# Attention units of one segment, two chunks at a time: a planned order laid out anew

## The chip, the cores and the metric

The kernel runs on one core of a Trainium2 chip. The metric is the device time of one execution in microseconds; several runs of a kernel are given by their median. A profile is taken of one further execution. The engines are named as in the profile: PE is the matrix engine, with its weight loads shown apart as PEld; DVE, ACT and POOL are the vector, scalar and general engines; SP issues nearly all DMAs.

## The reference

A sequence of 2048 rows of 512 goes through attention with a compressive memory and then through a gated feed-forward block, each behind a layer norm without weights and each with a residual:

```python
h  = x + attention(layernorm(x))          # wq, wk, wv, wo: 512 x 512, 32 heads of 16
h2 = h + ffn(layernorm(h))                # 512 -> 1376 -> 512, gelu(gate) * up
```

Attention works in four segments of 512 rows. Within a segment it is causal softmax attention. Each head also reads a memory of the earlier segments and then adds its own segment to it:

```python
a_dot = softmax(q k^T / 4 + causal mask) v
a_mem = (phi(q) M) / (phi(q) z + 1e-6)    # phi(t) = t + 1 for t > 0, else exp(t)
o = g * a_mem + (1 - g) * a_dot           # g = sigmoid(beta), one per head
M, z = M + phi(k)^T v, z + sum(phi(k))    # after each of the segments
```

So segment s of a head needs the memory that segment s-1 of the same head left. All is in float32.

## The kernel before

**Precision.** A large product is made of three: each operand is split into a rounded high part and a low part, and high-high, high-low and low-high are summed (`SPLIT`). Weights are split on ACT (high part) and on POOL or DVE (low part) by `split_weight` and `split_wv`.

**Units.** Eight heads form a chunk `c` (0 to 3). The 16 units of attention are the pairs (chunk, segment), and `UNITS` lists them in the order in which they are worked. Before, the first half takes chunk 0 with segments 0 and 1, chunk 1 with segments 0 and 1, and so on; the second half does the same with segments 2 and 3. For each unit `qkv(U)` projects q and k (24 matmuls, L653; for unit 0 both together at L665), splits them on ACT (L735) and DVE (L739), and moves the parts by DMA into the layouts that the score products want: three DMAs of q (L750) and six of k (L756) per half unit, issued by SP. `vproj` (L694) makes v for two chunks at a time, in the units whose chunk is even. If a later segment wants the memory, `qkv` also makes phi(k) (L673 to L677), transposes it (L773), multiplies it with v (L781) and adds it up (L788 to L796). `mem(U)` reads the memory for segments above 0: the denominator (L811), its inverse on DVE (L817 to L819), the product (L827) and the multiplication (L829).

**Passes.** A unit has two halves of four heads, numbered Q = 2U and 2U + 1. `pass_a(Q)` computes scores with queries on the rows (L855) for their maxima alone, which DVE takes out of the banks (L863); the maxima are transposed (L886), copied (L889) and written by a small DMA into the q operand (L891). `pass_b(Q)` computes the scores again with keys on the rows and the maxima subtracted by the product itself (L920, L928), ACT takes the exponential (L936), POOL cuts the triangle (L939), and PE multiplies with v in four column strips (L960). The result is copied (L981), goes through HBM, is divided and joined with the memory's part (L984 to L1006), and goes to `o_dram`.

**What sets the order.** The whole program is written out by a list planner, `Sched.run`, as the kernel is built. Each step is an operation with an engine, a duration, a priority, and the values that it reads and writes; buffers and banks come from pools. The planner takes the step that can begin first and, among those that can begin within 0.059 us of it, the one of the lowest priority. The priorities come from the unit's number plus a due time of each step out of the table `DUE` ("q", "k", "d", "v", "m" per unit; "a", "b", "p", "o" per half; "w" for the output projection and "l" for the first layer norm per segment). The real engines then run their instructions in that order and wait where data is late.

**Written over the plan by hand.** In some places the code issues an instruction at another place than the planner put it. `AHEAD` names five halves whose maxima DMA is marked `urgent`: it is issued ahead of the next DMA of SP once it is possible. `BEHIND` places the first squares of a later layer norm on ACT behind the high part of the first k. The steps of the first layer norm are fused so that the root on ACT and the final normalisation stand where they were wanted. `again` puts up to six matmuls of 512 columns, whose result isn't used, into pass B of the last half (L1116).

**The start.** The rows of segment 0 are loaded and normalised, while 17 transposes whose result isn't used run on PE (L533). The rows are transposed (L602), unit 0's q and k are projected, then v. In the order before, unit 1 is chunk 0 of segment 1, so segment 1's layer norm and its transposes (L613) come right behind. The layer norms of segments 2 and 3 are laid out with units 4 and 5 (`LN1_AT`).

**The end.** `wo_seg` projects a segment's output once all four chunks of it are done (L1033). The second layer norm and the feed-forward products (L1220, L1285) follow; they take over the banks and buffers of attention as these come free.

The weights of the next chunk are split once a unit of an odd segment has been laid out:

```python
        if s % 2 and U < 15:
            h, cn = divmod(U // 2 + 1, NCH)
            for i in range(2):
                W[h, cn, i] = split_weight(2 * (U + 1) + (-3.175), (wq, wk)[i][cn], PW)
            if c % 2:
                split_wv(h, cn // 2, 2 * (U + 1) - 2.4, 3.0)
```

Of the kernel before, what the change touches and what calls it, by code (L numbers as in the profile page):

```python
# [15 lines left out]
P = 128  # L16
D = 512
# [11 lines left out]
UNITS = [(c, s) for h in range(2) for c in range(NCH) for s in (2 * h, 2 * h + 1)]  # L29
# [107 lines left out]
class Sched:  # L137
# [4 lines left out]
    def __init__(self):  # L142
        self.ops, self.urgent = [], set()
# [28 lines left out]
    def run(self, window=0.059, stay=0.1):  # L172
# [5 lines left out]
        while cand:  # L178
# [72 lines left out]
def infini_geglu(ctx: ExitStack, tc: tile.TileContext, x, wq, wk, wv, wo, beta,  # L251
# [29 lines left out]
    def dma(prio, fn, ins, outs, kb=256, dur=None, **k):  # L281
        return S.op("SP", dur or (0.4 if kb == 256 else 0.64), prio, fn, ins, outs, lat=kb / 290, **k)
# [79 lines left out]

    vh = Val(PE_)
# [3 lines left out]
    def c_iota():  # L367

        nc.gpsimd.memset(ones[:, 0:1], 1.0)
        nc.scalar.activation(ones[:, 1:2], ones[:, 0:1], AF.Sqrt)  # L370
# [18 lines left out]
    dve(1000, -9.5, c_mmask, [vh, vj], [vmmask, vh, vj])  # L389
# [7 lines left out]
    pool(0.5, -9, c_ident, [], [vident])  # L397
# [7 lines left out]
    vone, vq0, vk0, vv0 = Val(), [Val() for _ in stq_t], [Val() for _ in stk_t], [Val() for _ in va_t]  # L405

    pool(0.7, -8.5, lambda: None, [vident], [vone])
# [20 lines left out]
    def c_stk(i, after):  # L428
        t = stk_t[i]
        for a in range(2):  # L430
            own, other = slice(64 * a, 64 * a + 64), slice(64 - 64 * a, 128 - 64 * a)
            def fill(a=a):

                if i == 1:
                    if a:
                        nc.scalar.activation(ones[:, 1:2], ones[:, 0:1], AF.Exp)
                    return
                for s, b in [(i, a)] + ([(1, 0), (1, 1)] if i == 0 and a else []):
                    rows = slice(64 * b, 64 * b + 64)
                    nc.scalar.activation(stk_t[s][rows, :, b], one[rows, :, None].to_broadcast([64, 2, D]), AF.Copy)  # L440
            act(2 * D, -4.2 + i, fill, [vone] + after, [vk0[i]], src=0.1, chain=True)
# [32 lines left out]

    BEHIND = None


    def layer_norm(prio, rows, dst, off=False, keep=None, acq=None, done=(), behind=(), scratch=None):
        bn, mv = Val(PBN), Val(PMV)
        y, z = Val(PLN), Val(PLN)  # L480
# [15 lines left out]
        for t in range(4):  # L496
            if off:
# [10 lines left out]
                def squares(t=t, junk=junk):  # L508
                    nc.scalar.activation(junk.t, rows[t].t, AF.Square, bias=bn.t[:, t, 1:2],
                                         accum_out=mv.t[:, t, 1:2])  # L510

                def place(f=squares, late=t == 0 and BEHIND is None):

                    nonlocal BEHIND
                    if late and BEHIND is None:
                        BEHIND = f
                    else:
                        f()
                act(D, prio, place, [rows[t], bn], [junk, mv], src=0.4, chain=True)
            else:  # L520
                def f(t=t):
                    nc.vector.bn_stats(bn.t[:, t], rows[t].t)
                    nc.vector.bn_aggr(mv.t[:, t], bn.t[:, t])
                    if t == 3 and scratch and not behind:

                        nc.vector.tensor_scalar(v_(), mv.t[:, :, 1], 1e-5, None, op0=OP.add)
                        nc.scalar.activation(z.t, v_(), AF.Sqrt)
                dve(840, prio, f, [rows[t], *behind], [bn, mv], chain=True,
                    acq=[v, z] if t == 3 and scratch and not behind else [])
        if done and not behind:  # L530

            wm = Val(PB)
            pe(12 * 0.21, prio, lambda: [nc.tensor.transpose(  # L533
                wm.t[0:6, 0:P], ident[:, 0:6] if n else bn.t[:, 1], ident) for n in range(17)],
                [bn, vident], [wm])
# [17 lines left out]
        def y_():  # L553
            return y.t
        def z_():
# [8 lines left out]
        if done:  # L564
# [4 lines left out]
            n = 4 if behind else 3  # L569
            b = None if behind else Val(PLN)  # L570

            def root():
                nc.vector.reciprocal(y.t, z.t)
                nc.vector.scalar_tensor_tensor(b.t, mv.t[:, :, 0], -1.0, y.t, op0=OP.mult, op1=OP.mult)
                nc.scalar.activation(rows[3].t, rows[3].t, AF.Identity, scale=y.t[:, 3:4], bias=b.t[:, 3:4])
            dve(3500 if behind else 3250, prio, lambda: [
                *[f() for f in ([g, *[f for f, _, _ in steps]] if behind else [root])],
                *[norm(t) for t in range(n)]],
                [mv, *rows, *(HL0 if behind else [])], [v, u, y, z, *([b] if b else []), *rows[:n], *done])
            if b:  # L580
                act(4, prio, lambda: None, [b, y], [rows[3]])
# [17 lines left out]
        if done and not behind:  # L599
# [5 lines left out]
            for dc in range(ND):  # L605
                split_psum(prio, pts[dc], dst[dc])
            return
# [103 lines left out]
    def qkv(U):  # L711
# [11 lines left out]
        for i in range(2):  # L723
# [10 lines left out]
            def high(pm=pm, hl=hl, sc=sc, last=U == 0 and i == 1):  # L734
                nc.scalar.activation(hl.t[:, 0], pm.t, AF.Copy, scale=sc)  # L735
                if last:
                    BEHIND()
            act(D, first, high, [pm], [hl])
# [5 lines left out]
            for h, Q in enumerate(half):  # L744
                dst = (STQ, STK)[i][Q]
                zeros = (vq0, vk0)[i][Q:Q + 1]
                for r, part in enumerate(((0, 1, 0), (0, 0, 1))[i]):
# [6 lines left out]
                    for a in range(2):  # L754
                        dma(moved + 0.2 + h, lambda dst=dst, r=r, part=part, h=h, hl=hl, a=a:
                            nc.sync.dma_start(  # L756
                                dst.t[64 * a + r:64 * a + 64:4, :, a].bitcast(F32),
                                hl.t[64 * h + 32 * a:64 * h + 32 * a + 32, part].bitcast(F32)),
                            [hl] + zeros, [dst], kb=64, chain=True)
# [40 lines left out]
    def mem(U):  # L800
# [23 lines left out]
        spread(prio, r, U, 1, vr)  # L824
        pm = Val(PD)
        om = OM[U] = Val(POM)
# [4 lines left out]
    def spread(prio, r, U, i, vr):  # L831
# [3 lines left out]
            tensor=src.tensor, offset=src.offset, ap=[[0, 16], [D, 8], [1, D]])), [vr], [r], kb=430, dur=0.67)  # L835


    AHEAD = (12, 14, 18, 25, 29)


    def pass_a(Q):
# [51 lines left out]
        if Q in AHEAD:  # L893
            S.urgent.add(S.ops[-1].fn)

    def pass_b(Q):
# [14 lines left out]

        def bank(parts):
# [4 lines left out]
            def f():  # L917
                if kb == 3:
# [4 lines left out]
                    again(Q, kb)  # L923
# [6 lines left out]
                again(Q, kb)  # L930
# [174 lines left out]

    turns = []

    def again(Q, kb):
        if Q < 31 or kb == 0 or len(turns) == 6:
            return  # L1110
        turns.append(kb)
        f = forder[0]
        w, (v, c0) = FW[f], FWS[0, f]["a11"]
        assert banks_of[0, forder[1]][0].t is None
        dst = next(t for t in banks[3:5] if t is not banks_of[0, f][0].t)
        nc.tensor.matmul(dst[:w], v.t[:, 0, c0:c0 + w], B[0]["11"][0].t[:, 0, :], start=True, stop=True,  # L1116
# [271 lines left out]
```

## Time and profile before

| | us |
|---|---|
| median of 3 runs | 828.82 (828.08 to 829.05) |
| the profiled execution | 828.38 |
| its span in the profile | 826.7 |
| PE busy | 808.3 (98%) |
| DVE busy | 611.8 (74%) |
| ACT busy | 564.4 (68%) |
| POOL busy | 484.8 (59%) |

The span runs from the first to the last instruction on the engines; the profiled execution's own time is 1.7 us longer. Busy times of different engines overlap. A group of the profile gives the line, the engine, the operation, what is written and read, the shape and the count; behind the first bar the busy time and the mean length of one instruction in ns; behind the second the idle time of the engine just before them, and what ended it. Matmuls overlap one another, so the mean length of one is more than the distance between two. A line number can be that of a helper which several steps share.

### The profile page before, as it was taken

The numbers are of one execution on the slowest core, as the hardware profiler recorded it, in microseconds if no ns is written. First come the engines' busy times: TensorE is split into PE (matmuls) and PEld (weight loads), VectorE is DVE, ScalarE is ACT, GpSimd is POOL, SyncE is SP. The second block draws the span as 40 slices with busy tenths as digits, with TensorE's granted clock in tenths as the row PEclk, the third lists the DMA queues.
The fourth block names the chain that finished last, engine by engine and source line by source line (L and its number), as shares of the span: only waits on it lengthen the run. The fifth ranks groups of instructions, "written<-read, shape, count | busy, mean of one in ns | idle before, by whom it ended". The sixth has DMA issues, their size and how long they took to land.

```text
span 826.7 us, 15337 instructions
## 1 busy us (share of the span) xinstructions
PE 808.3 (98%) x4721; PEld 626.6 (76%) x4721; DVE 611.8 (74%) x1823; ACT 564.4 (68%) x1131; POOL 484.8 (59%) x720
## 2 busy tenths in 40 slices
PE   7999999999999999999999999999999999999998
PEld 6788777777867767867756587888888787888886
DVE  7889776888878878699985964666568865665665
ACT  8778788889787777876776753787467454546541
POOL 8433443443264454545736885888698676869750
PEclk9999999999999999999999999999999999999999
DMA  7543545655446655564654665431111341211202
GB/s 257 135 129 97 147 125 133 165 145 156 123 128 184 168 146 153 148 163 128 181 182 135 205 192 179 152 116 52 52 52 52 107 151 39 78 39 51 64 1 102
DMA packets 71893, 103.51 MB, mean 125 GB/s; under 512 B 14340, under 2 KB 25156, under 8 KB 71812
## 3 DMA queue, kind: packets, MB, share of 16 engines
q1 hardware_dynamic: 71668, 102.41, 42.4%
q8 instruction: 37, 0.61, 0.3%
q14 instruction: 44, 0.36, 0.1%
q10 hardware_dynamic: 144, 0.13, 0.0%
HBM read 54.92 MB, written 21.43 MB: 92 GB/s over the span
## 4 chain that ended last, share of the span: by engine, by line
PE 51%; DVE 3%; DMA 1%; ACT 1%; issue 0%; SPq 0%; POOL 0%; ACTq 0%; DVEq 0%
PE bank L1220 24%; PE bank L1285 14%; PE bank L1033 5%; PE bank L960 2%; PE bank L855 2%; PE bank L928 2%; PE bank L653 1%; DVE row L596 1%; PE bank L613 1%; DMA row<-o_dram 1%; DMA cd<-pv_dram 0%; DVE bank L1062 0%; PE bank L827 0%; DVE ln L551 0%; DVE aside L863 0%; ACT stk L1068 0%
## 5 line engine op out<-in xcount | busy, mean ns | idle before, releaser
L939 POOL TENSOR_SCALAR_AFFINE_SELECT pt<-pt 128x128 f32<-128x128 f32 (+2 forms) x352 | 119.9, 349 | 173.7 <-ACT pt L936 168.8
L936 ACT ACTIVATE pt<-bank 128x512 f32<-128x512 f32 (+1 forms) x352 | 182.5, 558 | 40.5 <-PE bank L928 28.1
L863 DVE CUSTOM_DVE_ANT_0 bank<-bank,amask 128x512 f32<-128x512 f32 (+1 forms) x256 | 156.7, 637 | 32.2 <-PE bank L855 30.7
L855 PE MATMUL bank<-stk,stq 128*128 128x512 f32 (+2 forms) x384 | 131.1, 383 | 3.4 <-DVE nm L863 2.1
L928 PE MATMUL bank<-stq,stk 128*128 128x384 f32 (+2 forms) x384 | 114.5, 354 | 2.2 <-ACT pt L936 2.1
L653 PE MATMUL bank<-xt,w 128*128 128x512 f32 x360 | 102.9, 395 | 0.0
L855 PEld LDWEIGHTS bank<-stk,stq 128*128 128x128 f32 x384 | 69.2, 188 | 26.6 <-DVE nm L863 10.0
L1293 DVE TENSOR_TENSOR pt<-pt,bank 128x512 f32<-128x512 f32 x95 | 64.1, 686 | 33.0 <-PE bank L1285 33.0
L863 DVE CUSTOM_DVE_ANT_0 aside<-bank,amask 128x256 f32<-128x256 f32 (+1 forms) x256 | 76.7, 353 | 14.8 <-PE bank L855 13.6
L928 PEld LDWEIGHTS bank<-stq,stk 128*128 128x128 f32 x384 | 68.0, 188 | 22.8 <-ACT pt L936 9.0
L960 PE MATMUL bank<-pt,vaug 128*32 128x512 f32 (+3 forms) x1024 | 76.7, 436 | 0.0
L653 PEld LDWEIGHTS bank<-xt,w 128*128 128x128 f32 x360 | 65.2, 188 | 10.1 <-DVE xt L623 0.2
L960 PEld LDWEIGHTS bank<-pt,vaug 128*32 128x32 f32 x1024 | 28.7, 109 | 40.9 <-issue 33.8
L863 DVE DVE_READ_ACCUMULATOR2_ANT nm<- 128x1 f32 x512 | 57.0, 111 | 0.0
L694 PE MATMUL bank<-wv,xt 128*128 128x256 f32 x384 | 55.0, 282 | 0.0
L694 PEld LDWEIGHTS bank<-wv,xt 128*128 128x128 f32 x384 | 51.9, 189 | 1.6 <-DVE mb L790 0.2
L455 POOL TENSOR_TENSOR w<-raw,w 128x512 fp32r<-128x512 f32 x25 | 32.3, 1293 | 29.6 <-ACT w L450 21.5
L1220 PE MATMUL bank<-xt,w 128*128 128x512 f32 (+1 forms) x168 | 46.5, 394 | 0.0
L1190 POOL TENSOR_TENSOR stk<-raw,stk 128x512 fp32r<-128x512 f32 (+3 forms) x28 | 31.1, 1111 | 22.8 <-PE bank L1220 14.5
L1190 POOL TENSOR_TENSOR w<-raw,w 128x512 fp32r<-128x512 f32 (+3 forms) x34 | 38.7, 1142 | 4.3 <-ACT w L1188 3.5
L1220 PE MATMUL bank<-xt,stk 128*128 128x512 f32 (+1 forms) x138 | 38.1, 391 | 0.3 <-ACT pq L1227 0.3
L1220 PE MATMUL bank<-stk,w 128*128 128x512 f32 (+1 forms) x135 | 38.0, 391 | 0.0
(310 smaller groups left out, 1847.7 us busy)
## 6 DMA issues: line engine op xcount, KB each, us to landing
stq<-hl SPq DMA_DIRECT2D x96, 128.0 KB
stk<-hl SPq DMA_DIRECT2D x192, 64.0 KB
pv_dram<-pvs SPq DMA_DIRECT2D x32, 256.0 KB
r<-r_dram SPq DMA_DIRECT2D x28, 256.0 KB
row<-x SPq DMA_DIRECT2D x24, 256.0 KB
raw<-wg SPq DMA_DIRECT2D x20, 256.0 KB
raw<-wu SPq DMA_DIRECT2D x20, 256.0 KB
raw<-wd SPq DMA_DIRECT2D x20, 256.0 KB
```

Of the source, the lines that this page charges most:

```text
L653: nc.tensor.matmul(pm.t, w.t[:, wi, dc * P:(dc + 1) * P], XT[s][dc].t[:, xi, :], start=dc == 0 and n == 0, stop=dc == ND - 1 and n == 2)
L694: nc.tensor.matmul(pm.t[:, 256 * t:256 * t + 256], XT[s][dc].t[:, xi, t0:t0 + P], whl[wi].t[:, h, 256 * (dc % 2):256 * (dc % 2) + 256], st ...
L855: nc.tensor.matmul(sa.t[:, k * w:(k + n) * w].rearrange("x (n w) -> x n w", n=n), sq.t[:, p, i * P:(i + 1) * P], sk.t[:, p, a:a + n, 0:w], ...
L863: nc.vector.tensor_tensor_reduce(out=(sa.t if i > 1 else aside)[:, k * w:(k + 1) * w], in0=sa.t[:, k * w:(k + 1) * w], in1=amask[:, D - w: ...
L928: nc.tensor.matmul(sc.t[:, lo:lo + D - q0], sk.t[:, p, a, q0:q0 + P], sq.t[:, p, q0:D], start=True, stop=True)
L936: act(w, prio, lambda: nc.scalar.activation(e.t[:, :w], sc.t[:, :w], AF.Exp), [sc], [e])
L939: nc.gpsimd.affine_select(v, v, pattern=pat + [[1, P]], compare_op=OP.is_ge, fill=0.0, base=0, channel_multiplier=-1)
L960: nc.tensor.matmul(pv.t[32 * n:32 * n + 32, kb * P:D], va.t[:, 136 * kb + 17 * j:136 * kb + 17 * j + 32], e.t[:, lo:lo + D - kb * P], star ...
L1190: pool(0.14 + 2.13e-3 * (hi - lo), prio, lambda: nc.gpsimd.tensor_tensor(v.t[:, 1, :hi - lo], r.t[:, lo:hi], v.t[:, 0, :hi - lo].bitcast(F ...
L1220: nc.tensor.matmul(dst.t[:w], v.t[:, wi, c0 + j * w:c0 + (j + 1) * w], b[bk][j].t[:, xi, :], start=first and j == 0 and n == 0, stop=j == ...
L1285: nc.tensor.matmul(pm.t[:, cs], HH[p, f, s][hi].t[:w, t * P:(t + 1) * P], v.t[:w, wi, cs], start=f == fl[0] and n == 0, stop=f == fl[-1] a ...
L1293: dve(W_, prio, lambda a=a, pm=pm, cs=cs, to=to: nc.vector.tensor_tensor(to.t[:, cs], a.t[:, cs], pm.t[:, cs], op=OP.add), [pm, a], [to])
```

## The change

`UNITS` takes two chunks of one segment, then the same two chunks of the next segment, then the other two chunks. The table `DUE` is another one throughout. Several durations that the planner reckons with are set to other values: a DMA of less than 256 KB holds SP for 0.68 rather than 0.64, the mask and the identity at the start take longer. What was written over the plan by hand is gone: `urgent`, `AHEAD`, `BEHIND`, and the fused steps of the first layer norm, which are steps of their own now, as are the two loads of ACT's function tables (`vtab`). The fills of the k operands of the first two halves are four ACT steps of one half tile each. For Q = 0, the four DMAs of k's high part (part 0) are issued by ACT, through `by_act`. The dummies at the start are 20 transposes that wait for the second row tile. The fillers in the last pass B are up to ten matmuls of 512 columns, one behind each group of score products once a bank is free. The multiplied memory read's buffer `om` is taken when the denominator is spread, not at the product. Weights are split when the next unit is the first of its chunk in this half.

```diff
-UNITS = [(c, s) for h in range(2) for c in range(NCH) for s in (2 * h, 2 * h + 1)]
+UNITS = [(c, s) for h in range(2) for p in (0, 2) for s in (2 * h, 2 * h + 1) for c in (p, p + 1)]
...
 DUE = {
-    "q": [-4, -4, 1.75, 2.5, 4, -3.75, 2.375, 1.25, 2.25, 4, 1.875, 3.875, 3.5, -3.5, 0.75, 4],
+    "q": [4, 0.25, -0.375, -0.625, 1.875, 2, 0, 2.25, 0.5, 4, 1.375, 4, 1, -2.875, -2.5, 4],
...
-    "l": [0, 0, -1.625, 0.375],
+    "l": [0, 0, 1.75, -0.75],
 }
...
-            if o.eng == "SP":
-
-                for q in cand:
-                    if q.fn in self.urgent:
-                        self.urgent.remove(q.fn)
-                        q.fn()
-                        q.fn = int
-            self.urgent.discard(o.fn)
             o.fn()
...
-        return S.op("SP", dur or (0.4 if kb == 256 else 0.64), prio, fn, ins, outs, lat=kb / 290, **k)
+        return S.op("SP", dur or (0.4 if kb == 256 else 0.68), prio, fn, ins, outs, lat=kb / 290, **k)
+
+    def by_act(prio, fn, ins, outs):
+        S.op("ACT", 0.45, prio, lambda: fn(nc.scalar), ins, outs, lat=2.4, chain=True)
...
-            pe(12 * 0.21, prio, lambda: [nc.tensor.transpose(
-                wm.t[0:6, 0:P], ident[:, 0:6] if n else bn.t[:, 1], ident) for n in range(17)],
-                [bn, vident], [wm])
+            pe(20 * 0.213, prio, lambda: [nc.tensor.transpose(
+                wm.t[0:24, 0:P], (ident if n else rows[1].t)[:, 0:24], ident) for n in range(20)],
+                [rows[1], vident], [wm])
...
+                        def move(eng, dst=dst, r=r, part=part, h=h, hl=hl, a=a):
+                            eng.dma_start(dst.t[64 * a + r:64 * a + 64:4, :, a].bitcast(F32),
+                                          hl.t[64 * h + 32 * a:64 * h + 32 * a + 32, part].bitcast(F32))
+                        if Q == 0 and part == 0:
+                            by_act(prio + 0.2, move, [hl] + zeros, [dst])
+                        else:
+                            dma(moved + 0.2 + h, lambda move=move: move(nc.sync), [hl] + zeros, [dst], kb=64,
+                                chain=True)
...
-    AHEAD = (12, 14, 18, 25, 29)
+    fills = []
...
-        if Q in AHEAD:
-            S.urgent.add(S.ops[-1].fn)
...
+        def fill():
+
+
+            if Q == 31 and PX.free and len(fills) < 10:
+                fills.append(Q)
+                nc.tensor.matmul(PX.free[0][2], sk.t[:, 0, 0, 0:P], sq.t[:, 0], start=True, stop=True,
+                                 skip_group_check=True)
...
-        if s % 2 and U < 15:
-            h, cn = divmod(U // 2 + 1, NCH)
+        if U < 15 and UNITS[U + 1][1] % 2 == 0:
+            cn, h = UNITS[U + 1][0], UNITS[U + 1][1] // 2
             for i in range(2):
                 W[h, cn, i] = split_weight(2 * (U + 1) + (-3.175), (wq, wk)[i][cn], PW)
-            if c % 2:
+            if cn % 2 == 0:
                 split_wv(h, cn // 2, 2 * (U + 1) - 2.4, 3.0)
```

More of the change, by code (lines that the diff above doesn't have):

```diff
@@ L360, in infini_geglu @@
     vident, vamask, vmmask, vgt = (Val() for _ in range(4))
+    vtab = Val()
+    pool(0.1, -9.7, lambda: nc.gpsimd.memset(ones[:, 0:1], 1.0), [], [vtab])
+    act(1, -9.7, lambda: nc.scalar.activation(ones[:, 1:2], ones[:, 0:1], AF.Sqrt), [vtab], [vtab], src=1.4)
     vh = Val(PE_)
@@ L396, in c_ident @@
             nc.gpsimd.tensor_tensor(one, one if i else ident[:, 3:4], ident[:, r:r + 1], op=OP.add)
-    pool(0.5, -9, c_ident, [], [vident])
+    pool(1.2, -9, c_ident, [], [vident])
     vcalm = [Val(), Val()]
     vz3 = [Val() for _ in q3_t]
-    vone, vq0, vk0, vv0 = Val(), [Val() for _ in stq_t], [Val() for _ in stk_t], [Val() for _ in va_t]
-    pool(0.7, -8.5, lambda: None, [vident], [vone])
+    vq0, vk0, vv0 = [Val() for _ in stq_t], [Val() for _ in stk_t], [Val() for _ in va_t]
     def c_fill():
@@ L431, in c_stk @@
             own, other = slice(64 * a, 64 * a + 64), slice(64 - 64 * a, 128 - 64 * a)
[L432 to L441, printed above, removed]
+            act(2 * D, -4.3 if i < 2 else -4.2 + i, lambda a=a, own=own: nc.scalar.activation(
+                t[own, :, a], one[own, :, None].to_broadcast([64, 2, D]), AF.Copy),
+                [vident] + (after if i > 1 else []), [vk0[i]], src=0.14, chain=True)
             pool(0.93, -4.2 + i, lambda a=a, other=other: nc.gpsimd.memset(
@@ L507, in layer_norm @@
                     chain=True)
[L508 to L519, printed above, removed]
+                act(D, prio, lambda t=t, junk=junk: nc.scalar.activation(
+                    junk.t, rows[t].t, AF.Square, bias=bn.t[:, t, 1:2],
+                    accum_out=mv.t[:, t, 1:2]), [rows[t], bn], [junk, mv], src=0.4, chain=True)
             else:
@@ L523, in f @@
                     nc.vector.bn_aggr(mv.t[:, t], bn.t[:, t])
[L524 to L529, printed above, removed]
+                dve(840, prio, f, [rows[t], *behind], [bn, mv], chain=True)
         if done and not behind:
             wm = Val(PB)
-            pe(12 * 0.21, prio, lambda: [nc.tensor.transpose(
-                wm.t[0:6, 0:P], ident[:, 0:6] if n else bn.t[:, 1], ident) for n in range(17)],
-                [bn, vident], [wm])
+            pe(20 * 0.213, prio, lambda: [nc.tensor.transpose(
+                wm.t[0:24, 0:P], (ident if n else rows[1].t)[:, 0:24], ident) for n in range(20)],
+                [rows[1], vident], [wm])
         def g():
@@ L568, in norm, with inv @@
                                         op0=OP.subtract, op1=OP.mult)
[L569 to L581, printed above, removed]
+            if behind:
+                dve(3500, prio, lambda: [*[f() for f in [g, *[f for f, _, _ in steps]]], *[norm(t) for t in range(4)]],
+                    [mv, *rows, *HL0], [v, u, y, z, *rows, *done])
+            else:
+                b = Val(PLN)
+                dve(94, prio, lambda: nc.vector.tensor_scalar(
+                    v_(), mv.t[:, :, 1], 1e-5, None, op0=OP.add), [mv], [v])
+                act(4, prio, lambda: nc.scalar.activation(z.t, v_(), AF.Sqrt), [v], [z], src=0.17)
+                def inv():
+                    nc.vector.reciprocal(y.t, z.t)
+                    nc.vector.scalar_tensor_tensor(b.t, mv.t[:, :, 0], -1.0, y.t, op0=OP.mult, op1=OP.mult)
+                dve(280, prio, inv, [z, mv], [y, b])
+                dve(1320, prio, lambda: [norm(t) for t in range(3)], [y, mv, *rows[:3]], [*rows[:3], *done])
+                act(4, prio, lambda: nc.scalar.activation(
+                    rows[3].t, rows[3].t, AF.Identity, scale=y.t[:, 3:4], bias=b.t[:, 3:4]),
+                    [b, y], [rows[3]], src=0.7)
         else:
@@ L606, in layer_norm @@
                 split_psum(prio, pts[dc], dst[dc])
+            act(1, prio, lambda: nc.scalar.activation(ones[:, 1:2], ones[:, 0:1], AF.Exp),
+                [vtab, dst[3]], [vtab], src=1.4)
             return
@@ L733, in qkv @@
             sc = 0.25 if i == 0 else 1.0
[L734 to L738, printed above, removed]
+            act(D, first, lambda pm=pm, hl=hl, sc=sc: nc.scalar.activation(
+                hl.t[:, 0], pm.t, AF.Copy, scale=sc), [pm], [hl])
             dve(D, first, lambda pm=pm, hl=hl, sc=sc: nc.vector.scalar_tensor_tensor(
@@ L754, in qkv @@
                     for a in range(2):
[L755 to L759, printed above, removed]
+                        def move(eng, dst=dst, r=r, part=part, h=h, hl=hl, a=a):
[3 more added lines that the diff above has]
+                            by_act(prio + 0.2, move, [hl] + zeros, [dst])
+                        else:
+                            dma(moved + 0.2 + h, lambda move=move: move(nc.sync), [hl] + zeros, [dst], kb=64,
+                                chain=True)
                 if i == 0 and Q >= len(stq_t):
@@ L922, in f @@
                             k3.t[:, p], q3.t[:, p], start=True, stop=True)
-                    again(Q, kb)
+                    fill()
                     return
@@ L929, in f @@
                                      sq.t[:, p, q0:D], start=True, stop=True)
-                again(Q, kb)
+                fill()
             if kb == 3:
@@ L1102, in ln2 @@
                        acq=[[y, t] for y, t in zip(ys, ts)] + [[], []], scratch=scratch)
[L1106 to L1116, printed above, removed]
-                         skip_group_check=True)
     ln1(0)
```

18 lines of the change are left out of this document (8 added, 10 removed), and 30 rows, old and new, of the table DUE.

## The prediction

> **What bounds the kernel now.** I read the page's head first, then the busy time by stage, then what the matrix engine (PE) does in the attention stage, then the chain of waits for the rate of work in which nothing waits.
>
> ```profile
> span 826.7 us, 15337 instructions
> PE 808.3 (98%) x4721; PEld 626.6 (76%) x4721; DVE 611.8 (74%) x1823; ACT 564.4 (68%) x1131; POOL 484.8 (59%) x720
> ```
> ```profile
> 26.40:466.30 439.90, 432.47 (x3022) 320.40 (x3020) 358.93 (x1384) 343.32 (x719) 205.51 (x429) 1.00 0.52 146
> 466.30:823.00 356.70, 355.64 (x1585) 289.94 (x1581) 232.10 (x385) 199.76 (x376) 258.14 (x246) 1.00 0.29 92
> ```
>
> The columns after the length of a stage are the busy times of PE, PE's weight loads, DVE, ACT and POOL, then the granted clock. PE is busy for 98% of the span at a granted clock of 1.00. From 466.3 on it idles 1.1 of 356.7 us, so a new layout can take nothing there. Attention (26.4 us, the first score product, to 466.3 us, the last copy of a P·V result) shows 7.4 us of idle PE. But a PE that is called busy can still run its matmuls one by one, each waiting a little. So I count the stage's work at the rate of undisturbed runs. The groups of that stage:
>
> ```profile
> L855 PE MATMUL bank<-stk,stq 128*128 128x512 f32 (+2 forms) x384 | 131.1, 383 | 3.4 <-DVE nm L863 2.1 <-DMA stq<-hl 0.3 <-DMA stk<-hl 0.2
> L928 PE MATMUL bank<-stq,stk 128*128 128x384 f32 (+2 forms) x384 | 114.5, 354 | 2.2 <-ACT pt L936 2.1
> L653 PE MATMUL bank<-xt,w 128*128 128x512 f32 x360 | 102.9, 395 | 0.0
> L960 PE MATMUL bank<-pt,vaug 128*32 128x512 f32 (+3 forms) x1024 | 76.7, 436 | 0.0
> L694 PE MATMUL bank<-wv,xt 128*128 128x256 f32 x336 | 49.1, 282 | 0.0
> L1033 PE MATMUL bank<-w,wv 128*128 128x512 f32 x48 | 13.8, 396 | 0.0
> L920 PE MATMUL bank<-q,k 128*128 128x256 f32 x64 | 13.8, 296 | 0.4 <-ACT pt L936 0.3
> L781 PE MATMUL bank<-vaug,pkn 128*128 128x136 f32 x96 | 13.1, 279 | 0.0
> L827 PE MATMUL bank<-pq,mb 128*128 128x512 f32 x24 | 12.2, 591 | 0.0
> L613 PE MATMUL bank<-ident,row 128*128 128x128 f32 x60 | 8.6, 274 | 1.1 <-DVE row L596 1.1
> L773 PE MATMUL bank<-ident,pk 128*128 128x128 f32 x48 | 7.2, 273 | 0.0
> L1033 PE MATMUL bank<-wv,wv 128*128 128x512 f32 x24 | 7.0, 398 | 0.0
> L1033 PE MATMUL bank<-xt,wv 128*128 128x512 f32 x24 | 6.9, 394 | 0.0
> L811 PE MATMUL bank<-pq,mb 128*32 128x128 f32 x96 | 5.0, 279 | 0.0
> L1116 PE MATMUL bank<-xt,w 128*128 128x512 f32 x6 | 2.4, 397 | 0.0
> ```
>
> The rates, from the chain (start, length, what):
>
> ```profile
> 356.20 2.29 PE bank L960 x32
> 374.72 0.93 PE bank L781 x8
> 537.60 12.95 PE bank L1220 x57
> 630.24 1.31 PE bank L613 x12
> ```
>
> A 512-column matmul costs 12.95/57 = 0.227 us, hence 384 columns 0.170 and 256 columns 0.114 by proportion; a transpose of 128 columns 0.109. Pass A (L855) has per half unit six products of 512, four of 384, two of 256; pass B (L928) has four of each. So there are 192 + 128 + 360 + 96 + 24 = 800 of 512 columns (182 us), 256 of 384 (44), 64 + 128 + 64 + 336 = 592 of 256 (67), 32 runs of L960 (73), 12 runs of L781 (11), 108 transposes and 96 small L811 (about 16): 393 us. The stage lasts 440. **About 47 us are loss**: 7 seen as idle, 40 hidden, where one product stands between two waits or PE changes between the full array (L855) and column strips (L960). Some of it is the cost of changing and no layout removes it; the rest is all that this change can win or lose in the middle.
>
> **The change part by part.** The number of projections, passes, transposes, splits, and DMAs of attention stays the same; the pairing only reorders them. What differs in number: six filler matmuls of 512 columns become up to ten, the start-up dummies go from 17 to 20 transposes, four DMAs are issued by ACT rather than SP.
>
> *The start up to the first real transposes (8.7 us).* The dummies run while the first layer norm is under way; rows:
>
> ```profile
> 5.28 3.62 PE L533 MATMUL bank<-ident 128*6 128x128 f32 x16
> 8.69 2.21 PE L602 MATMUL bank<-ident,pt 128*128 128x128 f32 x16
> 4.30 0.66 DVE L522 BATCH_NORM_STATS2 bn<-pt 128x6 f32<-128x512 f32 x1
> ```
>
> Sixteen dummies take 3.62 us, 0.226 each, twenty 4.5. They now wait for the second row tile itself, which has landed by 4.30 (its statistics begin there), not for the statistics; they end near 8.8, as before. I put 0, bounds −0.3 and +0.8 (three more dummies behind a late row). The norm's chain and its four fills on ACT keep their kind and count.
>
> *From 16 us to 40 us.* Unit 1 is now chunk 1 of segment 0, not chunk 0 of segment 1, so it doesn't need the second layer norm.
>
> ```profile
> 17.63 1.93 SPq L750 DMA_DIRECT2D stq<-hl  x3
> 19.65 4.55 SPq L756 DMA_DIRECT2D stk<-hl  x6
> 22.97 1.60 PE L613 MATMUL bank<-ident,pt 128*128 128x128 f32 x4 [0.56 <-DVE pt L567]
> 24.85 1.80 PE L613 MATMUL bank<-ident,pt 128*128 128x128 f32 x12 [0.27 <-DVE pk L677]
> 26.40 0.71 PE L855 MATMUL bank<-stk,stq 128*128 128x512 f32 x2
> 35.11 0.50 PE L855 MATMUL bank<-stk,stq 128*128 128x512 f32 x1 [0.40 <-DVE nm L863]
> 20.00 2.55 POOL L455 TENSOR_TENSOR w<-raw,w 128x512 fp32r<-128x512 f32 x2
> ```
>
> Before, PE stands still 0.56 and 0.27 us for that norm and 0.40 us in pass A. The weights of chunk 1 are split by 22.55 even before the change (the POOL row), so unit 1's 24 matmuls (5.4 us) are ready just when PE used to wait. Four of the six key DMAs of the first half go to ACT: SP is done 4 × 4.55/6 = 3.0 us earlier, and pass A starts at about 23.4. Both take the same 1.2 us of idle, so I count it once: −1.2, bounds −3.0 (if pass B, too, is pulled in by all of it) and 0. ACT pays four issues. No row shows one on ACT; SP's 0.76 is the nearest, so 3.0 us, and 0 if they overlap. What hides it is vproj on PE; without that cover the copies of its banks come late, +1.5. The second layer norm stays, and its DVE work now falls beside pass A; unit 2 needs its result one unit later than unit 1 did (a unit lasts 440/16 = 27.5 us).
>
> The Trainium skill ("DMA: Bandwidth & Descriptors", section "Issuing engines are not separate DMA queues") says that issuing from several engines saves only the sequencer's time and that this is usually small beside the transfer. Read strictly it makes the earlier issue worth nothing. By it this term would be −0.8, the norm's two waits alone. The rows have 6.5 us of issue in the 8.8 between 17.63 and 26.40, so here issue is most of it.
>
> *The middle.* This can't be worked out instruction by instruction, since the due times (DUE) are all new. Bounds come from the 47 us of loss: a tenth of the hidden 40 is 4 us, and I take −8 and +6 as far ends. For a gain speaks that a unit's memory products (L811, L827) now wait on results two units back, not one, and that vproj falls on every other unit evenly. Against it: five row-max DMAs were moved ahead by hand (AHEAD), and that is dropped. ACT's wait for such DMAs is
>
> ```profile
> ACT q L909 <- DMA stq<-mx: 8.4, 7, 3.4
> DVE bank L863 <- PE bank L855: 30.2, 39, 4.1
> ```
>
> (total, times, longest); it isn't PE's, so I count +0.6, bounds 0 and +3. Between ends so far apart the nearest rows are the waits of PE that the groups L855 and L928 name, 3.4 and 2.2 us; I take a little under half of these 5.6, −2.5, for the rest of the middle.
>
> *The end of attention.* The six fillers (L1116, 2.4 us) stand in pass B's waits for ACT; ten cost up to 4 × 0.227 = 0.9 more, or nothing where they stand in such waits as the six do. Segment 2 is complete after unit 13 rather than 14, so its output projection can fill PE in the last unit. −0.6, bounds −2 and +1.
>
> Sum: 0 − 1.2 + 0.6 − 2.5 − 0.6 = −3.7. The profiled execution took 828.38 us (span 826.7 and 1.7 around it), 0.4 under the median of 828.82; 828.38 − 3.7 = 824.7, and with the 0.4 the forecast is **825.1 us**; its own range is 821 to 827.
>
> **The rivals.**
>
> *The gaps only move (no change).* In the second row above DVE waits 30 us for PE while PE's products wait for banks that DVE and ACT drain: a ping-pong with a fixed number of turns per half unit. If these turns make the hidden 40 us, the pairing leaves them and just the start's 1.2 is won, less the 0.6 lost: 828.2. Against: the loss should then be alike in all stages of the middle, and a tight stage like the start loses little.
>
> *Heavy pairs (slower).* Units with segment above 0 carry the memory read. Its DVE rows:
>
> ```profile
> L818 DVE RECIPROCAL bank<-bank 128x128 f32<-128x128 f32 x12 | 11.6, 966 | 0.4
> L819 DVE TENSOR_SCALAR z<-bank,gt 128x128 f32<-128x128 f32 x12 | 4.2, 351 | 0.4
> L829 DVE TENSOR_TENSOR om<-bank,r 128x512 f32<-128x512 f32 x12 | 8.2, 687 | 1.2 <-PE bank L827 1.2
> L677 DVE SCALAR_TENSOR_TENSOR pq<-bank,e 128x512 f32<-128x512 f32 x12 | 8.2, 684 | 0.5 <-ACT e L675 0.4
> ```
>
> That is 0.97 + 0.35 + 0.69 + 0.68 = 2.7 us per unit. Before, units without and with it alternate in the first half; now two light ones and two heavy ones follow each other (2, 3 and 6, 7). Over the stage DVE idles 440 − 359 = 81 us, 5 per unit. If the heavy pair's 5.4 us meet a DVE that is already full (pass A follows pass A), PE waits for most of it: about 2 us in each of units 2, 3, 6, 7, less the start's gain and the rest: 828.8 + 5 − 1 = 832.5. It decides where DVE idles less than 2.7 us per unit. Against it speak the 5 us of mean slack.
>
> *SP's queue (slower).* Without AHEAD the row-max DMAs stand behind others in SP's order, each up to ACT's longest wait of 3.4 us; at five places a third of it on PE's path is 5.7 us, less the start's 1.2 and the middle's 2.5: 828.8 + 2.0 = 831.
>
> **How the numbers follow.** A difference under 0.2% (1.7 us) can't be told from none here. Forecast 0.50 (825.1); gaps only move 0.20 (828.2); heavy pairs 0.16 (832.5); SP's queue 0.14 (831). Faster: most of the first, 0.50 with the low part of the second and less the upper tail of the first; within 0.2%: 0.20; slower: 0.30. The range leaves out a tenth on each side: below, a middle that wins the far end of −8 (828.8 − 10 = 819); above, 832.5.
>
> **What would show it.** PE's idle time between 16 and 40 us falls from 1.2 to about 0, and the first L855 starts near 23.4. The busy counts per group stay as they are, fillers aside. The stage from the first score product to the last copy of P·V takes some 2 to 4 us less, and from there to the end the time is unchanged within 1 us. The forecast is wrong if that stage is longer; heavy pairs would show as L855 waiting for DVE in units 2, 3 and 6, 7 (by 27.5 us a unit from 26.4 about 81 to 136 us and 191 to 246 us), the queue as ACT's waits for stq<-mx growing beyond 8.4 us with PE waits behind them, and a lost start as new waits of PE for weights before 40 us.

## The result and the profile after

The changed kernel takes 822.17 us (median; 821.09 to 824.37), the kernel before in the same series 828.45 us. The ratio is 0.993, 95% interval 0.9913 to 0.9948: **6.3 us faster**, where 3.7 were forecast (825.1, with a range of its own of 821 to 827 and a whole one of 819 to 832.5). Lines of the changed file lie some 14 to 30 lower: pass A is L835 (before L855), pass B L914 and L906, the product with v L946, the projections L634, v L675.

The head of the page after, and the busy time by stage (length, then PE, PE's weight loads, DVE, ACT, POOL, granted clock, DMA):

```profile
span 820.5 us, 15349 instructions
PE 805.0 (98%) x4728; PEld 629.1 (77%) x4728; DVE 615.2 (75%) x1823; ACT 561.7 (68%) x1131; POOL 483.8 (59%) x720
```
```profile
25.59:462.50 436.91, 431.02 (x3039) 323.84 (x3037) 365.64 (x1392) 346.24 (x729) 208.24 (x432) 1.00 0.53 149
462.50:816.70 354.20, 353.91 (x1577) 289.02 (x1574) 229.56 (x377) 195.26 (x369) 255.51 (x245) 1.00 0.29 90
```

The span is 6.2 us shorter, and three stages make it: attention begins 0.8 us earlier (25.6 for 26.4), lasts 3.0 less (436.9 for 439.9), and the rest is 2.4 shorter (358.0 from 462.5 to the end, 360.4 before). The last is partly work moved across the boundary: the rows above show 1577 matmuls behind it and 1585 before, 8 × 0.227 = 1.8 us; PE's idle time there fell from 1.1 to 0.3.

Within attention the gain lies late. Three windows of both kernels, before first (PE's time and count come first):

```profile
81.00:136.00 55.00, 54.95 (x427) 42.16 (x429) 38.68 (x147) 43.81 (x93) 23.70 (x56) 1.00 0.49 132
191.00:246.00 55.00, 54.08 (x376) 41.62 (x374) 46.97 (x188) 45.17 (x96) 24.01 (x52) 1.00 0.46 128
246.00:356.00 110.00, 108.89 (x790) 79.94 (x789) 86.91 (x330) 86.02 (x181) 54.69 (x118) 1.00 0.58 161
```
```profile
81.00:136.00 55.00, 54.45 (x397) 41.81 (x396) 42.46 (x177) 40.57 (x86) 19.86 (x50) 1.00 0.47 124
191.00:246.00 55.00, 55.00 (x417) 43.94 (x417) 48.70 (x195) 47.19 (x102) 21.73 (x53) 1.00 0.58 163
246.00:356.00 110.00, 109.56 (x808) 82.36 (x807) 86.26 (x339) 86.44 (x183) 54.65 (x115) 1.00 0.51 142
```

Between 81 and 136 us PE idles 0.5 us more than before, from 191 to 356 it idles 1.6 less. The counts of a window can't be compared directly, since the order of the units differs and with it the mix of matmuls. So I count each matmul of both traces at the prediction's rates (fillers and dummies at nothing); this is an estimate. By it the changed kernel's work is 0.8 us ahead at 26 us, 0.3 behind at 44, 2.3 behind at 136, 1.8 ahead at 246, 3.9 at 356 and 5.6 at 440. What attention gains by its earlier beginning is spent by 44 us, and the gain comes behind 136.

What ended PE's idle time and its late weight loads at pass A's line, first before, then after (total, times):

```profile
  DVE nm L863: 12.1, 32
```
```profile
  DVE nm L843: 4.7, 18
```

**Pass A's weight loads and products wait 7.4 us less for DVE to take the maxima out of a bank.** Most of this is wait of the weight loads, which can pass while PE is still busy. DVE's line names the two apart, before and after:

```profile
  PEld bank L855: 10.0, 28
  PE bank L855: 2.1, 4
```
```profile
  PEld bank L835: 4.5, 17
  PE bank L835: 0.2, 1
```

Pass B's group went the other way, 114.5 to 117.2 us of busy time:

```profile
L835 PE MATMUL bank<-stk,stq 128*128 128x512 f32 (+2 forms) x384 | 127.0, 374 | 0.6 <-DVE nm L843 0.2
L914 PE MATMUL bank<-stq,stk 128*128 128x384 f32 (+2 forms) x384 | 117.2, 359 | 2.1 <-ACT pt L922 2.0
```

### The profile page after: what moved, and what is told of

It is laid out like the page before. It is cut to its first block, busy times and chain, and to the rows that moved or that the text cites. A ratio compares the mean times of both kernels' runs of the same rounds, so it can differ in the third digit from the quotient of the medians.

```text
span 820.5 us, 15349 instructions
## 1 busy us (share of the span) xinstructions
PE 805.0 (98%) x4728; PEld 629.1 (77%) x4728; DVE 615.2 (75%) x1823; ACT 561.7 (68%) x1131; POOL 483.8 (59%) x720
## 4 chain that ended last, share of the span: by engine, by line
PE 88%; POOL 4%; DVE 4%; ACT 2%; issue 1%; DMA 1%; SPq 0%; POOLq 0%; ACTq 0%; DVEq 0%
PE bank L1191 23%; PE bank L1256 14%; PE bank L634 10%; PE bank L835 9%; PE bank L946 8%; PE bank L914 8%; PE bank L675 5%; PE bank L1019 5%; PE bank L762 1%; PE bank L808 1%; PE bank L594 1%; DVE bank L843 1%; PE bank L906 1%; POOL raw L1168 1%; DVE row L575 1%
## 5 line engine op out<-in xcount | busy, mean ns | idle before, releaser
L835 PE MATMUL bank<-stk,stq 128*128 128x512 f32 (+2 forms) x384 | 127.0, 374 | 0.6 <-DVE nm L843 0.2
L914 PE MATMUL bank<-stq,stk 128*128 128x384 f32 (+2 forms) x384 | 117.2, 359 | 2.1 <-ACT pt L922 2.0
L634 PE MATMUL bank<-xt,w 128*128 128x512 f32 x360 | 102.5, 396 | 0.1
L914 PEld LDWEIGHTS bank<-stq,stk 128*128 128x128 f32 x384 | 68.0, 189 | 22.0 <-ACT pt L922 7.8
L835 PEld LDWEIGHTS bank<-stk,stq 128*128 128x128 f32 x384 | 68.7, 188 | 18.8 <-DVE nm L843 4.5
L946 PE MATMUL bank<-pt,vaug 128*32 128x512 f32 (+3 forms) x1024 | 76.9, 436 | 0.0
L634 PEld LDWEIGHTS bank<-xt,w 128*128 128x128 f32 x360 | 65.1, 188 | 10.5 <-DVE xt L604 0.4
L946 PEld LDWEIGHTS bank<-pt,vaug 128*32 128x32 f32 x1024 | 28.8, 109 | 40.2 <-issue 32.4
L675 PE MATMUL bank<-wv,xt 128*128 128x256 f32 x384 | 55.6, 283 | 1.1 <-POOL wv L459 1.1
L675 PEld LDWEIGHTS bank<-wv,xt 128*128 128x128 f32 x384 | 52.4, 189 | 3.4 <-POOL wv L459 1.3
L443 POOL TENSOR_TENSOR w<-raw,w 128x512 fp32r<-128x512 f32 (+1 forms) x28 | 36.1, 1296 | 26.1 <-ACT w L438 25.9
L1161 POOL TENSOR_TENSOR w<-raw,w 128x512 fp32r<-128x512 f32 (+3 forms) x30 | 35.1, 1170 | 15.8 <-ACT w L1159 7.8
L1191 PE MATMUL bank<-xt,w 128*128 128x512 f32 (+1 forms) x159 | 43.5, 390 | 0.0
L967 ACT ACTIVATE pvs<-bank 128x512 f32<-128x512 f32 x32 | 19.2, 599 | 26.1 <-PE bank L946 15.1
```

Source lines behind the costliest of these rows:

```text
L634: nc.tensor.matmul(pm.t, w.t[:, wi, dc * P:(dc + 1) * P], XT[s][dc].t[:, xi, :], start=dc == 0 and n == 0, stop=dc == ND - 1 and n == 2)
L675: nc.tensor.matmul(pm.t[:, 256 * t:256 * t + 256], XT[s][dc].t[:, xi, t0:t0 + P], whl[wi].t[:, h, 256 * (dc % 2):256 * (dc % 2) + 256], st ...
L835: nc.tensor.matmul(sa.t[:, k * w:(k + n) * w].rearrange("x (n w) -> x n w", n=n), sq.t[:, p, i * P:(i + 1) * P], sk.t[:, p, a:a + n, 0:w], ...
L914: nc.tensor.matmul(sc.t[:, lo:lo + D - q0], sk.t[:, p, a, q0:q0 + P], sq.t[:, p, q0:D], start=True, stop=True)
L946: nc.tensor.matmul(pv.t[32 * n:32 * n + 32, kb * P:D], va.t[:, 136 * kb + 17 * j:136 * kb + 17 * j + 32], e.t[:, lo:lo + D - kb * P], star ...
L1161: pool(0.14 + 2.13e-3 * (hi - lo), prio, lambda: nc.gpsimd.tensor_tensor(v.t[:, 1, :hi - lo], r.t[:, lo:hi], v.t[:, 0, :hi - lo].bitcast(F ...
```

## The experiments

Three theories: T1, the order of the units makes the gain; T2, the searched due times make it, whatever the order; T3, what stands around them does (the start's measured durations, ACT's four DMAs, the patches dropped). Ratios are to the kernel before in the same series, with 95% intervals.

### The two orders without a table

```diff
-    "q": [4, 0.25, -0.375, -0.625, ...],
+    "q": [0, 0, 0, 0, ...],
...
-UNITS = [(c, s) for h in range(2) for p in (0, 2) for s in (2 * h, 2 * h + 1) for c in (p, p + 1)]
+UNITS = [(c, s) for h in range(2) for c in range(NCH) for s in (2 * h, 2 * h + 1)]
```

All entries of `DUE` are 0; the second kernel has the old order too.

> The changed kernel with every due time set to 0, so that the planner goes by the units' own order alone. Theory T1 (the order of the units makes the gain): it stays at least 4 us under the same kernel with the old order and due times 0. T2 (the searched due times make it): the two lie within 2 us of each other, both above 830. T3 (the code around it, the start's measured durations, ACT's DMAs, the patches dropped) says nothing of this pair.

> The changed kernel with the old order of units and every due time 0. T1: at least 4 us slower than the new order with due times 0. T2: within 2 us of it.

New order 832.09 us (1.0056, 1.0035 to 1.0076), old order 833.27 us (1.0065, 1.0044 to 1.0087). They differ by 1.2 us and the intervals overlap: T2's side. Its table is worth 10 us to the new order. Yet pass A's waits for DVE (it is L829 in these kernels) differ as in the result, first old, then new order:

```profile
  DVE nm L837: 14.5, 39
```
```profile
  DVE nm L837: 9.4, 33
```

### The old layout in the changed code, and the new table shaken

```diff
+DUE, UNITS = those of the kernel before        # first kernel
...
+DUE[k][i] += random.choice((-0.25, 0, 0.25))   # second kernel, seed 1
```

> The changed code with the old order of units and the old due times: only what stands around them is changed. T3: 822 to 825, most of the gain is there. T1 and T2: 827 to 833, no gain; above 828.8 if the dropped patches were worth something.

> The changed kernel with each due time moved at random by -0.25, 0 or +0.25. T1: the order holds the gain, 821 to 825. T2: a layout that was searched loses its gain when it is shaken, 826 or more.

857.81 us (1.0352, 1.0321 to 1.0383) and 869.46 us (1.0503, 1.0476 to 1.053). Neither number was within what any theory expected. The new table fits its code so closely that one random shake of a quarter unit costs 47 us, far more than having no table. One stage of the shaken kernel:

```profile
240.00:480.00 240.00, 224.46 (x1418) 152.86 (x1416) 172.94 (x646) 154.68 (x321) 109.43 (x220) 0.97 0.51 141
```

From 240 to 480 us PE idles 15.5 us and its granted clock is 0.97. The old layout's 30 us of loss in the new code therefore say nothing of the order, and nothing of T3 either, only that its table no longer fits. T3 gets no support: no kernel of the old order in the changed code, with no table or with one searched anew (below), is faster than the kernel before. The new order in the old code was not run.

### Both orders with equally searched tables

For each order a table was searched anew from zeros in the changed code, some 11,000 trials each, keeping changes that end the planner's own plan earlier (a table only; the code is the changed one). Two tables for the old order, one for the new.

```diff
-DUE = { ... }      # of the changed kernel
+DUE = { ... }      # searched anew; UNITS old, old, new
```

> The changed code with the old order of units and a table of due times searched anew for it: from zeros, some 11,000 trials that keep a change when the planner's own end of the plan is earlier. The pair with the next run has the same budget. T1 (the order makes the gain): 828 or more, and at least 3 us slower than the new order so searched. T2 (the search for the due times makes it): 822 to 827, and within 2 us of the new order.

> The changed code with the new order of units and a table searched from zeros with the same budget as the last run. T1: 822 to 825, at least 3 us under the old order. T2: within 2 us of the old order, and not far from the changed kernel, whose table is another one.

> The old order again in the changed code, with a second table that was searched from zeros on the same budget with other random trials. It tells the order from the luck of one search: if the order makes the 5.7 us between the last pair, this one too lies at 831 or more; if it was the luck of a table, it lies within 2 us of the new order's 827.5. If the old order's start lets the clock drop, its profile shows a granted clock under 0.95 in some stretch of the first 44 us.

Old order 833.2 us (1.0065, 1.0045 to 1.0085) and 830.53 us (1.0043, 1.0026 to 1.0061); new order 827.47 us (1.0001, 0.9984 to 1.0019). Both old ones are slower than the new one and the intervals don't touch: 0.42% and 0.64%, 3.5 and 5.3 us. The second falls between the bounds that were set for it (831 or more for T1, 829.5 or less for luck), nearer to T1's. T1's other condition, 822 to 825 for the new order, failed by 2.5 us, and T2's, the old order at 827 or less, by 3.5 or more. So **the table carries a part, and the order probably one**: after a search of equal length the new order is 3.5 to 5.3 us ahead, and the changed kernel's own table wins a further 0.71% (0.993 to 1.0001), 5.9 us, over the one searched here. But the new order had one searched table only, two tables of the old order differ by 0.22%, and without a table the orders could not be told apart, so a second table for the new order could still change the first number. How this splits with a table as long searched for the old order stays open; the kernel before is one such in the old code (828.45), but with its own patches and durations.

Pass A's waits, in the order of the numbers above:

```profile
  DVE nm L837: 13.9, 29
```
```profile
  DVE nm L837: 13.7, 27
```
```profile
  DVE nm L837: 11.4, 33
```

At equal tables, none or equally searched, the old order waits more here than the new one (14.5 to 9.4; 13.9 and 13.7 to 11.4). But the wait doesn't rank the times: the new order without a table has 9.4 at 832.09 us, and the kernel before with AHEAD emptied (below) has

```profile
  DVE nm L863: 9.2, 28
```

at no measurable gain of the median over 12.1 (its profiled execution, 825.14 us, was its fastest). The profiled executions don't carry the difference of the medians either: the old order's took 832.09 and 829.87 us and the new order's 830.71, which is 3.2 above its median. So this wait goes with the order at equal tables, but that it makes the 6.3 us or a part of them isn't shown.

The clock differs too. The first kernel of the old order, from 16 us on in steps of 4 us (the clock is the third number from the end):

```profile
16.00:20.00 4.00, 2.94 (x21) 2.58 (x20) 0.77 (x4) 1.09 (x3) 3.92 (x8) 1.00 0.24 72
20.00:24.00 4.00, 3.36 (x18) 3.16 (x18) 3.14 (x13) 2.39 (x6) 2.93 (x3) 0.66 0.74 186
24.00:28.00 4.00, 3.65 (x27) 3.22 (x26) 2.86 (x8) 3.39 (x8) 2.08 (x3) 0.92 0.75 196
```

Here the granted clock falls for a while (the first score product follows at 26.9 us), and the changed kernel holds 1.00 in these windows. The second kernel of the old order holds it there too and loses it at 470 to 480 us:

```profile
470.00:480.00 10.00, 8.37 (x22) 6.06 (x23) 8.97 (x16) 5.95 (x12) 6.27 (x5) 0.66 0.44 149
```

So the expectation of a clock drop at the old order's start held in one of two. At the end of attention the first old kernel loses the clock once more, and the new order with its searched table loses it there as well; first old, then new:

```profile
460.00:470.00 10.00, 8.68 (x58) 4.80 (x56) 7.84 (x16) 5.22 (x10) 6.55 (x11) 0.83 0.22 59
```
```profile
460.00:470.00 10.00, 8.70 (x58) 4.98 (x58) 7.32 (x12) 5.20 (x11) 5.77 (x7) 0.83 0.33 97
```

Counted as time lost at full rate, which is an estimate (length times what is missing to 1.00), that is 3.4 us in each of the two old kernels and 1.7 in the new one. Over all executions the mean granted clock was 0.992 to 0.998 in the 14 of the old order, with a median of 0.996 for each of its two kernels, and 1.0 in seven of the new order's ten. The missing 0.4% are 3.3 us, so the clock may be most of the order's 3.5 to 5.3 us. The new order's other three executions had 0.998 and took 1.0030 to 1.0035 of the kernel before; the second old kernel's at 0.998 took 1.0014 to 1.0052, so at the same clock these two can't be told apart. The changed kernel's own 6.3 us are not this: 20 executions of the kernel before had 1.0, over all series, and none of them was under 824.53 us.

### The start

Three kernels keep the changed kernel's planned order and touch its first 26 us. The first has SP issue the four DMAs that ACT issues:

```diff
-        S.op("ACT", 0.45, prio, lambda: fn(nc.scalar), ins, outs, lat=2.4, chain=True)
+        S.op("ACT", 0.45, prio, lambda: fn(nc.sync), ins, outs, lat=2.4, chain=True)
```

> The changed kernel in the same planned order, but the four DMAs of k's high part for the first half are issued by SP where the plan had ACT issue them. If the issue by ACT carried part of the gain (as the prediction had it, up to 1.2 us at the start), this is 1 to 3 us slower than the changed kernel, with the first score product 2 to 3 us later than 25.6. If PE has enough other work there, it is within 1 us.

823.68 us (0.9943, 0.9925 to 0.9961). The first score product comes at 26.22 rather than 25.59 us, not 2 to 3 us later. The 0.13% (1.1 us) over the changed kernel lie within the intervals: a small gain of the issue by ACT can't be told from none.

The second makes a low part of v's weights on DVE; the third also puts the first squares behind the high part of k, as the kernel before had it:

```diff
-            pool(1.23, prio, lambda r=r, k=k: nc.gpsimd.tensor_tensor(
+            first = h == cp == 0 and k == 1
+            pool(1.23, prio, lambda r=r, k=k, first=first: (nc.vector if first else nc.gpsimd).tensor_tensor(
```

> The changed kernel in the same planned order, but the low part of the second half of the first v weights is made by DVE (0.7 us, DVE waits there anyway) and not by POOL behind a fill of 0.95 us. If PE's wait of 1.1 us for that part is what ate the start's gain: PE's idle there goes to 0 and the time falls by about 1 us, ratio to the kernel before 0.2 points of a per cent lower. If the next wait takes its place (the q and k parts come no earlier), the time stays within 0.4 us of the changed kernel.

> As the last one, and the first squares of the third segment's layer norm stand behind the high part of the first k on ACT, as in the kernel before. If the dropped patch made the first parts late: q's and k's high parts end 0.9 us earlier than 18.9, the first score product starts near 24.7 rather than 25.6, and the time is 1 to 2 us under the changed kernel. If PE has other work there, the same time as the last one.

822.61 us (0.9937, 0.9916 to 0.9958) and 823.06 us (0.9948, 0.993 to 0.9966), no gain. PE in the second and in the third kernel:

```profile
19.61 3.14 PE L676 MATMUL bank<-wv,xt 128*128 128x256 f32 x24 [0.60 <-DVE hl L718]
22.90 0.98 PE L635 MATMUL bank<-xt,w 128*128 128x512 f32 x3 [0.15 <-ACT vaug L687]
25.58 0.70 PE L836 MATMUL bank<-stk,stq 128*128 128x512 f32 x2
```
```profile
24.06 0.96 PE L645 MATMUL bank<-xt,w 128*128 128x512 f32 x3 [1.72 <-ACT vaug L697]
26.64 0.71 PE L849 MATMUL bank<-stk,stq 128*128 128x512 f32 x2
```

The wait for POOL is gone, and one for DVE stands in its place; the first score product comes at the same 25.58. In the third it comes at 26.64, where 24.7 was expected: PE waits 1.72 us for ACT's copy out of v's bank, which ACT reaches late: its queue is held by the DMAs that it issues.

```profile
19.24 0.64 ACTq L748 DMA_DIRECT2D stk<-hl  x1
19.91 2.09 ACTq L748 DMA_DIRECT2D stk<-hl  x1
22.03 1.27 ACTq L748 DMA_DIRECT2D stk<-hl  x2
23.35 0.66 ACT L697 ACTIVATE vaug<-bank 128x256 f32<-128x256 f32 x2 [3.05 <-issue]
```

This is the prediction's "+1.5 without that cover", seen. With the patch back SP begins its DMAs of q at 18.04 us, and the first score product is still 1 us later than without it:

```profile
18.04 1.93 SPq L742 DMA_DIRECT2D stq<-hl  x3
```

At the start the gaps only move.

### The fillers, and the row-max DMAs moved by hand

```diff
-            if Q == 31 and PX.free and len(fills) < 10:
+            if Q == 31 and PX.free and len(fills) < 0:      # changed kernel
...
-    AHEAD = (12, 14, 18, 25, 29)
+    AHEAD = ()                                             # kernel before
```

> The changed kernel without the ten filler matmuls in the last pass B; their result isn't used. If they stand in waits that PE has anyway: within 0.5 us of the changed kernel, and PE's waits for ACT there longer by their 2 to 3 us. If they cost: up to 3 us faster.

> The kernel before without the five maxima DMAs issued ahead by hand; the plan is the same otherwise. If that patch was worth what the prediction feared for its loss (0.6, at most 3 us on PE's path, 5.7 in the rival of SP's queue), this is 1 to 5 us slower than the kernel before. If the DMAs are off PE's path: within 0.5 us.

Without fillers 823.43 us (0.9938, 0.9918 to 0.9959): they cost nothing that can be measured. From 450 to 460 us, after with them and then without:

```profile
450.00:460.00 10.00, 8.24 (x47) 5.26 (x49) 7.62 (x13) 8.09 (x17) 7.19 (x13) 1.00 0.51 160
```
```profile
450.00:460.00 10.00, 8.00 (x34) 5.09 (x34) 7.47 (x12) 7.57 (x17) 7.00 (x14) 0.83 0.49 150
```

With 13 matmuls fewer PE is busy nearly as long: the granted clock is 0.83, and each takes longer. PE's waits for ACT at pass B didn't grow by the 2 to 3 us that were expected; they are 2.0 us in both.

Without AHEAD the kernel before takes 827.59 us (1.0018, 0.9992 to 1.0043; its times go from 825.14 to 834.14): inconclusive, and nothing like the 5.7 us of the rival.

## Why the prediction was right or wrong

**Direction and range held; the size was 60% of what came**, and the sum's parts were wrong in opposite ways.

*The start up to 8.7 us*, put at 0: the first real transposes come at 8.91 for 8.69 us, within its bounds.

*16 us to 40 us*, put at −1.2: **this step failed.** From 16 to 44 us PE idles 1.6 us as before, where its idle time was to go to about 0, and it does 0.3 us less work by the estimate above; before first, then after:

```profile
16.00:44.00 28.00, 26.38 (x171) 22.57 (x170) 23.47 (x83) 21.11 (x44) 14.05 (x19) 1.00 0.51 131
```
```profile
16.00:44.00 28.00, 26.41 (x155) 21.60 (x154) 23.89 (x87) 20.02 (x40) 11.23 (x19) 1.00 0.51 126
```

The norm's waits did go, but the prediction took the removed patches for free here and asked only what ACT's issue wins. PE, ACT and SP after:

```profile
18.68 4.46 PE L675 MATMUL bank<-wv,xt 128*128 128x256 f32 x35 [1.08 <-POOL wv L459]
```
```profile
17.12 0.71 ACT L494 ACTIVATE junk<-row,bn 128x512 f32<-128x512 f32 x1
17.83 1.06 ACT L715 ACTIVATE hl<-bank 128x512 fp32r<-128x512 f32 x2
18.92 0.63 ACTq L734 DMA_DIRECT2D stk<-hl  x1
20.21 2.04 ACTq L734 DMA_DIRECT2D stk<-hl  x2
```
```profile
19.07 3.17 SPq L728 DMA_DIRECT2D stq<-hl  x3
22.34 1.60 SPq L734 DMA_DIRECT2D stk<-hl  x2
```

Without BEHIND the squares stand ahead of q's and k's high parts, so SP begins at 19.07 rather than 17.63; three DMAs of q hold SP 3.17 us rather than 1.93 while ACT issues too; a new wait of 1.08 us for POOL takes the place of the norm's 0.83. Of the 3.0 us that the first score product was to come earlier, 0.8 are left, and by 44 us nothing. The strict reading of the Trainium skill ("DMA: Bandwidth & Descriptors", "Issuing engines are not separate DMA queues"), by which the earlier issue is worth nothing, was nearer in number than the term made from the rows; the run with SP issuing can't tell it from a small gain.

*The middle*, −2.5 and +0.6: **pass A was the right place, the size was too small, and the reasons given aren't shown.** Behind the first score product the span lost 5.4 us, where the sum had 2.5 for middle and end. The term was sized as a little under half of the 5.6 us of idle PE that pass A and pass B named. Late weight loads, which the prediction counted only within its hidden 40 us, hold more than that idle: pass A's waits for DVE were 12.1 us with them, and 7.4 of these went, while pass B's group grew by 2.7. The reasons given, that the memory products (L811, L827) wait on results further back and that vproj (L694) falls evenly, had little to win on PE itself, which stood idle 0.0 us before each of them in the prediction's own rows. Why DVE comes to the maxima in better time stays open. No run takes these waits away by themselves, so their share of the gain isn't known. The +0.6 for AHEAD didn't come: ACT's wait for the row-max DMAs, 8.4 us before, is

```profile
ACT q L887 <- DMA stq<-mx: 2.9, 3, 1.2
```

*The end*, −0.6: the extra fillers cost nothing, as put. "Unchanged within 1 us" behind attention was wrong: 2.4 us less, about 1.8 of it work that had moved ahead of the boundary.

*The rivals.* That the gaps only move is right for the start and wrong for the middle. Heavy pairs: between 81 and 136 us PE idles 0.5 us more than before, for 191 to 246 it idles 0.9 less, and DVE's 55 − 48.7 = 6.3 us of idle in the second of these leave 3.1 per unit, above the 2.7 where the rival decides. By the estimate above work does fall 2.0 us behind from 44 to 136 us, but not by the wait that the rival names: pass A's waits for the maxima fell in both windows, 0.7 to 0.2 and 0.8 to 0.5 us. So it fell. Its sum was also off: 828.8 + 5 − 1 is 832.8, not 832.5. SP's queue fell with ACT's wait. That the change would be lost because one code's table doesn't fit another's was no rival, and would have been the dearest, at 30 to 47 us.

*The count of the loss.* The 393 us leave out the 32 transposes of the maxima (L886) and the six fillers, together some 5 us at the same rates (an estimate), so the loss is nearer to 42 than to 47 us. No term of the sum hangs on it, only the far ends set for the middle.

## What to carry to other kernels

Where a planner's table of due times has been searched, order, durations and table are one thing: change one and the table must be searched again, or no table at all is the better start (832 against 858 to 869 us here). When you size what a new layout can win, look at the late weight loads and the waits of one producer and consumer pair too, not only at the idle time that the matrix engine shows; but such a wait alone did not rank the kernels here. Before a profile is taken to explain a median, compare the profiled execution's own time with it. And when patches written over a plan are dropped with it, each is a term of the sum with its own place, even where it moved one instruction.

## What the runs showed of the hardware

*The clock falls without a long gap.* In the kernel without fillers PE's longest waits are these (total, times, longest):

```profile
PE bank L505 <- DMA pt<-x: 4.4, 1, 4.4
PE bank L914 <- ACT pt L922: 2.0, 5, 0.6
PE bank L594 <- DVE row L575: 1.8, 3, 1.1
```

The first is the start; behind it none is over 1.1 us, yet the granted clock is 0.83 in the window of 450 to 460 us, where PE is busy for 8.0 of 10. In three of four executions without the fillers the mean granted clock is 0.997 or 0.998, in the fourth 1.0; with the ten unused matmuls of 512 columns it is 1.0 in all four. The Trainium skill ("TensorE: Matmul & The Clock Gate", "Part 1: The HAM clock gate") gives about 3.4 us of an idle window as the condition for the half rate, and tells in the same part of a kernel whose many short idles made the clock swing. The rows here agree with the second: the drop comes without a gap of 3.4 us. How much idle is enough isn't shown. In the 3.4 us before this drop PE is busy for 2.08 us; in the kernel whose DMAs SP issues a stretch of the same length at 452 us has 2.09, and the clock stays at 1.00.

*DMA issues can take longer when two engines issue at once.* Nine DMAs of the first half unit take SP 6.57 us alone (17.63 to 24.20 before). With ACT issuing four of them the changed kernel takes 5.0 us, from 18.92 to 23.94; the second start kernel takes 3.9, from 18.86 to 22.76. Single issues on ACT take 0.60 to 0.64 us at their shortest and 2.09 at their longest (third start kernel), and SP's first three go from 1.93 to 3.17 us in the changed kernel but only to 2.05 in the second start kernel. What decides it stays open.
